# The same steps of a linear-attention and MLP-mixer kernel in another order of issue

## The chip, the cores and the metric

The kernel runs on one core of a Trainium2 chip. The metric is the device time in microseconds. The core has five instruction queues that each run strictly in their written order: TensorE (PE; its weight loads are shown as PEld), VectorE (DVE), ScalarE (ACT), GpSimd (POOL) and SyncE (SP), which here issues all DMA transfers. Semaphores tie the queues together.

## What is computed

The first half is a delta-rule recurrence over 768 tokens, for 4 batch elements with 8 heads of 48 features; the second is a mixer on its output. Cut to what matters:

```python
k_n = k / (norm(k, axis=-1) + 1e-06)
for t in range(S):                                    # 768 tokens
    y[:, :, t] = einsum('bhd,bhde->bhe', q[:, :, t], state)
    v_old = einsum('bhde,bhd->bhe', state, kt)
    state = state + bt[..., None] * einsum('bhd,bhe->bhde', kt, vt - v_old)
x = y.transpose(0, 2, 1, 3).reshape(B, S, H * D)      # (4, 768, 384)
h = maximum(x.transpose(0, 2, 1) @ w_tok1, 0) @ w_tok2   # 768 -> 256 -> 768
u = x + h.transpose(0, 2, 1)
out = u + maximum(u @ w_ch1, 0) @ w_ch2               # 384 -> 1536 -> 384
```

All data are float32 on the chip (the mixer's weights arrive as 64-bit floats and are rounded there).

## The kernel before

**Chunks.** The recurrence is done in chunks of 64 tokens: 12 per element, 48 in all (`r0` to `r47`). Two chunks make a unit `u` of 128 tokens (24 units). Inside a chunk the delta rule becomes the inverse of a triangular 64x64 matrix for each head, so that only the state goes from chunk to chunk. The inverses do not depend on the state and can be made ahead.

**Jobs and steps.** The kernel is written as some 280 Python generators, the jobs; each `next()` on one issues one step, a few instructions for one or two engines. A job's name is a letter and a number:

- `k` loads keys and queries of a unit (SP), `v` loads its values (SP) and scales them by the keys' norms on POOL (L426); a `v_st` tile has two buffers.
- `p` makes norms, scaled keys and the transposed keys and queries (`kq`); it uses ACT, DVE, POOL, and PE for units under 12; later units turn on DVE (L369).
- `c` and `d` are the grams `p_g` (PE L453) and their masking on DVE (L459).
- `t` hands the triangular blocks to the inversion. For the first six units engines copy them; later, four DMAs write them to `n_dram` (L628).
- `i0` to `i6` invert the 32x32 blocks of up to four units at once. From `i2` on its first step is a DMA that loads x from `n_dram` (L675); then come 30 steps of two DVE instructions, `sub` (L681) and `x` (L686), and the last one writes x to `w_dram` (L705). `f` fetches the inverses back (SP L653).
- `h` and `j` join the inverted blocks (PE `p_z`, `p_x`; ACT and DVE between).
- `r` is one chunk of the recurrence, ten steps numbered from 0: `p_k` from keys and state (PE L862, steps 0 to 3); `rest` = `p_k` - values (DVE L869, step 4); `p_y` and `p_w` (PE L882, L886, step 5); `w_t` (ACT L892, step 6); `p_s` and the rest of `p_y` (PE L900, L901, step 7); the new state `s_t` (DVE L909, step 8); the output (ACT L914, step 9). The first chunk of an element has no state and leaves out the first part.
- `m0` to `m3` are the mixers of the four elements: token matmuls `p_1` (PE L1060) and `p_h` (L1073), transposes `p_ut` (L1083), then for each of three pairs of token blocks the channel matmuls. For element 0 these are `p_c` (L1140, evicted by ACT); for the others a scheme with fewer products, `p_r` (L1032, evicted by ACT L1041 or added up by DVE L1044). The second channel matmul is `p_o` (L1162), added to the result by DVE (L1091) and stored by SP (L1094). The mixer has three PSUM tiles of its own.
- `w` loads and rounds pieces of the weights (SP, ACT, DVE, POOL), `s` forms sums of them on DVE, `b` loads beta, and `x`, `z` and `Y` are filler matmuls on zeros that write a PSUM tile of their own (L225, L235).

**The order.** A long string lists the steps: 2,543 of them, `name*n` for n steps in a row. A loop calls the jobs in that order, and since scheduling is manual, each engine's queue holds its instructions in exactly this order. So a step's place is its place on every queue that it uses: a `rest` listed behind a step of an inversion waits on DVE until that one is through. Tile buffers are given out and freed in this order too.

**What ties the order.** `r` of a chunk needs `j` of its unit (the joined inverse), `v` (scaled values) and the state of the chunk before. `m0` needs all twelve chunks of element 0 for its token matmuls, of which two chunks feed one step. `p` of unit u from 12 on overwrites the `kq` of unit u - 6, so it waits until the recurrence has read that. Assertions in the generators state these ties at build time.

Of the kernel before, what the change touches and what calls it, by code (L numbers as in the profile page):

```python
# [23 lines left out]
def kernel(  # L24
# [149 lines left out]
    t11 = const.tile([128, NB, HB], FP32, name="t11")  # L174
# [17 lines left out]
    w2 = const.tile([128, NDH, S], FP32, name="w2")  # L192
# [20 lines left out]
    def place(u):  # L213
        return NV + u if u < 2 else (u - 2) % NV
# [194 lines left out]
    def stacked(dst, src, u):  # L409
        rows = heads_of(src, u)  # L410
        for par in range(2):
            for cc in range(2):
                nc.sync.dma_start(
                    out=dst[PAR[par ^ cc], :, cc], in_=rows[par, cc]
                )
                yield

    def load_v(u):
        vsts[u] = v_st = loads.tile([128, NP, 2, D], FP32, name="v_st")
        yield from stacked(v_st, v, u)  # L420
        assert u in masked
        nrm = nrms[place(u)]
        nc.gpsimd.tensor_tensor(
            out=nrm, in0=nrm, in1=eps[:, :, None].to_broadcast([128, NP, 2]), op=ALU.add
        )
        nc.gpsimd.tensor_tensor(  # L426
            out=v_st, in0=v_st,
            in1=nrm[:, :, :, None].to_broadcast([128, NP, 2, D]), op=ALU.mult,
        )
        scaled.add(u)  # L430
        yield
# [121 lines left out]
    t16 = spare[:, cuts[1] : cuts[2]].rearrange("s (q t b) -> s q t b", q=2, t=QB)  # L553
# [688 lines left out]
    c1*2 d1 k2 p2*2 c1 t0 d1 c1*2 d1*3 t0 p2*8 c2*2 w2 d2 c2*3 Y d2 w2 k3*6 p3 d2*2  # L1242
    p3 d2 t1*3 x p3*7 c3 k4*5 k7 w13 w18*2 d3*2 v1*2 v0*2 c3*3 v0 c3 d3*3 t0 p4*2
    t2*3 x t3*2 p4*2 x t3 i0*2 w13 p4*2 w18 w17*2 i0 k4 i0*9 p4 i0*2 p4*2 c4 k8
    c4*3 w13*2 w6*2 k5*2 v0 k6 k5*2 i0*2 d4*2 k5 x z d4*3 c4 z*2 p5*2 k5 t4 p5 h0
    h1 h0 w8*2 h1 Y i0 f0 Y p4 f1 h2*2 p5*3 f0*2 w6 h0*5 k6*5 p6 z f2*2 k8*3 p5 w6
    p5 p3 p5 j0*3 f1*2 h1*5 j0*2 w8*2 w17 f2 h2*3 v0 t4*2 w17 r0*5 p6 h2*2 c5*2 v1
    w11*2 j1 p5 k7*2 c5 k7 c5 r0 c5 r0*2 w14*2 v1 w11*2 k7*2 p7 d5*5 r1*5 w14*2
    p6*2 t5 j1 t5*2 r1*2 j1 j2 p7 h3*2 r1*3 p6*3 i1*2 r2*5 k8*2 f3*2 w9 k9*3 j1*2
    v2*2 i1*3 j2*2 r2*2 f3 i1*2 p6*3 w16 v2 w16*3 r2*2 h3 r2 i1 d6 r3*5 i1*2 w9*3  # L1250
    v2 d6 h3 v2 w0 h3*2 r3 h3 d6*2 w0 d6 j3 c6*5 r3*4 w0 j2 w0 p8*2 j2 r4 p8 r4*4
    k9*3 j3*2 r4*2 i1*2 w24 i1*2 p7*7 r4 c7 r4 r5*5 k10 p9 k10 p9 c7 r4 c7*3 i1
    w5*2 p7 r5*2 w24*3 r5*3 j3*2 i1 r6*4 w26 v3*5 p9 k11 r6 d7*5 w26*3 p8*3 t6*2
# [8 lines left out]
    k12*3 m0*4 c10 m0*2 w25 m0 w12 d10 f6*4 f7*2 p11*2 m0*3 w12 w21 w12 p12 p11*2  # L1262
    m0*2 f7 w21*2 j6*2 j7 v6 p12 w25*3 f8*2 w27*2 m0 j6 j7*2 m0 r12*5 f8 f7 j8*2
    r12 m0 w23*4 j8 r12 t10 r12 t10*2 r13 p10 w23 r13*4 w20*2 p11*3 p12*2 w20*2
    f9*2 w32 f9 j9 f9 r13*2 f8 m0 r13 t10 r13 w31 w32 c11 w32 w23 w32 w31 p11 c11
    w31 d11 v8*3 r13 k13 c11 v8 c11*2 w30*2 w31 d11 r14 v8 d11 r14 d11*2 k13*6 r14
    t11 p12*2 k13 w29 r14*2 k13 m0 w30*2 k13*3 m0*4 r14*2 t11*2 c12*3 w29 c12*3 t12
    w33 r14*2 p12 t12 r14 t11 m0 w23 p13*3 r15 w25 t12*2 r15*4 m0 p13*3 k14*2 r15
    p13 r15 m0*4 k14*4 w33 k14*2 r15*3 c13*6 t13*2 w33 t13*2 i3 w31 r16*4 v9 k14*4
    w31 m0*2 r16 w33*3 j9 w27 v9 m0*2 j9 r16*2 w25 w31 m0 r16*2 j9 p14*3 r17*5 p14  # L1270
    r16 w33 m0 p14 k15*2 m0 v9 k15*2 i3*3 v10 i3 v9 m0*2 i3*3 m0*2 i3*2 p14 r17 p14
    i3 m0 i3 r17*4 i3 m0*6 i3*2 p13 i3*9 k15*3 j9 k15*2 p15 v9 i3*2 r18 i3 r18*2
    v10*2 k15*3 i3*5 r18*2 p15 v10 m0*2 f10*3 f11 m0*4 f11 m0*3 f11 f10 m0*4 r18
    f13*2 c14*6 f12*2 r18*4 m0*2 f12 m0 s p15 r19*5 j10 m0 r19*2 j10*2 s r19 p15*3
    r19*2 p14 f11 m0 j11*2 j12 r20 v10 r20*2 j11 r20*2 k16*6 p15 k16 m0*2 k16*2
    m0*2 r20 c15*2 k16*2 f13 r20 v11 c15*3 k16 v11 c15 v11 r20*3 p16 s v11 p16 m0*2
    r21*3 p15 r21*2 p16*4 j12 j13 k17*3 r21 j12 r21 p16 k17*3 m0*3 r21*3 m0 r22*2
    k17 r22 v11 k17 r22 k17*3 c16*4 r22*3 m0 c16*2 r22*3 t15 m0 r23*4 s p17*2 r23
    p16 p17*3 m0 p17 r23 k17 p17 t16 p17 m0*2 t16*2 t14*3 c17*2 t16 c17*3 r23 t14
    r23 c17 m0*2 s m0*3 t15*3 t17 s*4 t17*3 s*2 k18 m0*3 f12 i4*2 r23 i4*3 m0*2 i4  # L1280
    m0*2 v12*4 i4*2 k18 v12 k18*2 i4 k18 j13 m0*2 j13 r24*5 f13 j13*2 i4*4 r24 m0
    k18 m0*2 k18*2 v13*2 k18*2 r24 i4*2 k18*2 p18*2 i4 m0*3 r25 p18*2 r25*3 p18 i4
    k19 i4 k19 i4 k19*4 i4*2 m1 r25 m1*5 r24 r25 i4*8 k19*2 v14*4 i4 m1 v13*2 i4*2
    m1*2 p18*2 r25*2 m1 r25 m1 r25 p19*2 m1*3 r26*3 v13 r26*2 m1 c18*4 m1*2 r26*2
    m1*2 c18*2 m1*2 r26 m1 r26 m1*3 r27*2 k19*2 r26 k19*2 f14*3 r27*2 f14 j14*2
# [59 lines left out]
```

## Time and profile before

| what | value |
|---|---|
| runs of the kernel | 638.67, 640.15 and 643.08 us (median 640.15) |
| span of the profiled execution, first to last instruction | 636.9 us |
| PE busy | 608.5 us (96%), 9132 matmul passes |
| DVE busy | 447.9 us (70%) |
| ACT busy | 268.0 us (42%) |
| POOL busy | 107.2 us (17%) |
| mean granted clock of PE | 0.976 |
| DMA moved by the kernel's queue | 48.89 MB in 135,680 packets |

The profiled execution's time beside its span is not shown apart; the three runs are from 1.8 to 6.2 us longer than the span. In the profile a float32 matmul shows as two passes, a transpose as one. "Idle before" in brackets is how long an engine stood still before an instruction, and what released it. The granted clock (PEclk) is the share of PE's full speed in a stretch. A `q` behind an engine's name (SPq) is its instruction queue: issuing DMAs.

### The profile page before, as it was taken

The page shows a single profiled execution, that of the slowest core. Times are in us where ns is not written, and L with a number is a line of the kernel's source. Part 1 is how long each engine was busy: PE and PEld are TensorE (multiplying, and loading weights), DVE is VectorE, ACT ScalarE, POOL GpSimd, SP SyncE. Part 2 cuts the span into 40 slices and gives each one's busy share as a digit, 9 for nine tenths or more (in the row PEclk, how much of TensorE's full clock was granted, in tenths as well). Part 3 has the DMA queues.
Part 4 walks back from the last instruction along what each step waited for, and adds up shares of the span by engine and source line. Part 5 has one row for each costly group of instructions (what it writes and reads, how often), then busy time and mean ns, then how long its engine had stood idle before and what let it go on. Part 6 is the DMA issues. An engine that isn't in the chain of part 4 may idle for free.

```text
span 636.9 us, 21542 instructions
## 1 busy us (share of the span) xinstructions
PE 608.5 (96%) x9132; PEld 531.5 (83%) x9132; DVE 447.9 (70%) x1132; ACT 268.0 (42%) x693; POOL 107.2 (17%) x146
## 2 busy tenths in 40 slices
PE   8488988899999999999999999999999999999997
PEld 5367877668898988859889999769999987999997
DVE  4987876967999658988969987776728253373643
ACT  7758785447523342215624323325334130232240
POOL 2348354235210211111111001000010000000000
PEclk9978796999999999999999999999999999999999
DMA  9686666666543355344454223202020000000000
GB/s 201 127 148 151 153 142 153 162 135 162 110 113 89 71 116 101 76 109 79 90 103 95 43 82 58 48 5 42 5 53 2 27 2 0 26 1 26 2 26 26
DMA packets 135776, 50.27 MB, mean 79 GB/s; under 512 B 114656, under 2 KB 130144, under 8 KB 135680
## 3 DMA queue, kind: packets, MB, share of 16 engines
q1 hardware_dynamic: 135680, 48.89, 35.2%
q8 instruction: 72, 1.18, 0.8%
q14 instruction: 24, 0.20, 0.1%
HBM read 39.42 MB, written 9.44 MB: 77 GB/s over the span
## 4 chain that ended last, share of the span: by engine, by line
PE 82%; DVE 7%; ACT 4%; DMA 3%; issue 2%; POOL 1%; SPq 1%; ACTq 0%; DVEq 0%; POOLq 0%
PE p_o L1162 26%; PE p_r L1032 20%; PE p_c L1140 8%; PE p_h L1073 5%; PE p L1060 4%; PE p_k L862 3%; PE p_g L453 3%; PE p_y L882 3%; PE p_s L900 3%; PE p_w L886 1%; DVE sub L681 1%; DVE x L686 1%; PE p_y L901 1%; PE p_ut L1083 1%; PE p_z L785 1%
## 5 line engine op out<-in xcount | busy, mean ns | idle before, releaser
L1162 PE MATMUL p_o<-wc,r 128*128 128x192 f32 x720 | 126.1, 329 | 0.6 <-ACT u_t L1087 0.6
L1162 PEld LDWEIGHTS p_o<-wc,r 128*128 128x128 f32 x720 | 116.8, 190 | 2.7 <-ACT u_t L1087 1.1
L1044 DVE TENSOR_TENSOR r<-r,p_r 128x512 f32<-128x512 f32 x90 | 59.8, 684 | 38.1 <-PE p_r L1032 34.3
L1091 DVE TENSOR_TENSOR xb<-xb,p_o 128x192 f32<-128x192 f32 x84 | 29.3, 350 | 57.8 <-PE p_o L1162 57.3
L1041 ACT COPY r<-p_r 128x512 f32<-128x512 f32 x54 | 31.3, 585 | 85.7 <-PE p_r L1032 76.1
L686 DVE TENSOR_TENSOR x<-x,sub 128x84 f32<-128x84 f32 (+24 forms) x178 | 59.4, 334 | 6.1
L681 DVE TENSOR_TENSOR sub<-x 128x84 f32<-128x84 f32 (+24 forms) x178 | 58.0, 326 | 6.8 <-DMA x<-n_dram 2.3
L1162 PE MATMUL p_o<-wc,s 128*128 128x192 f32 x288 | 51.5, 331 | 0.3 <-DVE xb L1091 0.3
L1140 PE MATMUL p_c<-u_t,wc 128*128 128x256 f32 x216 | 51.0, 386 | 0.2 <-ACT u_t L1087 0.2
L1162 PEld LDWEIGHTS p_o<-wc,s 128*128 128x128 f32 x288 | 46.7, 190 | 1.4 <-DVE xb L1091 0.6
L1048 ACT ACTIVATE r<-r 128x512 f32<-128x512 f32 x54 | 34.0, 631 | 26.7 <-DVE r L1044 26.2
L426 POOL TENSOR_TENSOR v_st<-v_st,nrm 128x384 f32<-128x384 f32 x24 | 20.1, 838 | 146.3 <-DMA v_st<-in_v_dram 109.3
L1140 PEld LDWEIGHTS p_c<-u_t,wc 128*128 128x128 f32 x216 | 39.7, 190 | 6.0 <-ACT u_t L1087 0.4
L516 POOL TENSOR_TENSOR mb<-mask_c,cs 128x512 f32<-128x512 f32 x20 | 21.2, 1062 | 138.9 <-DVE cs L494 138.6
L914 ACT ACTIVATE xb<-p_y 64x192 f32<-64x192 f32 x96 | 31.2, 325 | 23.6 <-PE p_y L901 12.2
L892 ACT COPY w_t<-p_w 128x192 f32<-128x192 f32 x48 | 15.2, 316 | 58.0 <-PE p_w L886 57.5
L1032 PE MATMUL p_r<-u_t,wc 128*128 128x128 f32 x288 | 38.7, 277 | 0.0
L453 PE MATMUL p_g<-kq 48*64 48x128 f32 (+1 forms) x704 | 33.6, 281 | 3.8 <-ACT kq L529 3.3
L1032 PE MATMUL p_r<-t_d,wc 128*128 128x128 f32 x288 | 37.3, 280 | 0.0
L1032 PEld LDWEIGHTS p_r<-u_t,wc 128*128 128x128 f32 x288 | 35.3, 192 | 0.4
L1060 PE MATMUL p<-xb,w 128*128 128x384 f32 x96 | 34.9, 511 | 0.0
L1032 PEld LDWEIGHTS p_r<-t_d,wc 128*128 128x128 f32 x288 | 34.0, 192 | 0.8
(184 smaller groups left out, 1212.2 us busy)
## 6 DMA issues: line engine op xcount, KB each, us to landing
d<-in_moe_w_ch_dram SPq DMA_DIRECT2D x24, 384.0 KB, 3.5
v_st<-in_v_dram SPq DMA_DIRECT2D x96, 48.0 KB, 2.7
out_dram<-xb SPq DMA_DIRECT2D x23, 192.0 KB, 1.9
kst<-in_k_dram SPq DMA_DIRECT2D x64, 48.0 KB, 2.9
n_dram<-gm SPq DMA_DIRECT2D x72, 32.0 KB, 2.4
pads<-in_k_dram SPq DMA_DIRECT2D x24, 96.0 KB, 2.9
pads<-in_q_dram SPq DMA_DIRECT2D x24, 96.0 KB, 2.9
gm<-w_dram SPq DMA_DIRECT2D x72, 32.0 KB, 2.1
```

Source lines behind the costliest of these rows:

```text
L453: nc.tensor.matmul(p_g[PAR[i ^ cc], p], kqt[f, p, cc, 0], kqt[f, p, cc])
L681: nc.vector.tensor_tensor(out=tmp, in0=y[:, :, 0:s, s : s + 1].to_broadcast([n, k, s, w]), in1=y[:, :, s : s + 1, s + 1 : m].to_broadcast( ...
L686: nc.vector.tensor_tensor(out=y[:, :, 0:s, s + 1 : m], in0=y[:, :, 0:s, s + 1 : m], in1=tmp, op=ALU.add,)
L914: nc.scalar.mul(y[:, :, D * i : D * i + D], p_y[PAR[1 - i]], 1.0 if c else -1.0)
L1032: nc.tensor.matmul(p[:, i], pieces[i // width][:, at : at + 128], f[f"u{n}"], start=first and i == 0, stop=True, skip_group_check=True,)
L1041: nc.scalar.copy(o, p)
L1044: nc.vector.tensor_tensor(out=o, in0=o, in1=p, op=ALU.add if sign > 0 else ALU.subtract)
L1048: nc.scalar.activation(o, o, ACTF.Relu)
L1060: nc.tensor.matmul(p_1[dh], piece_of(w1, c, 0)[:, dh * 128 : (dh + 1) * 128], xb[:, c], start=(c == 0), stop=(c == NCH - 1),)
L1073: nc.tensor.matmul(p_h, piece_of(w2, j, c * 128)[:, c * 128 : (c + 1) * 128], r1[j], start=(j == 0), stop=(j == NDH - 1),)
L1140: nc.tensor.matmul(p_c[:, k], piece_of(wc1, cb, f * 128)[:, f * 128 : (f + 1) * 128], u_t[:, cb], start=(cb == 0), stop=(cb == NCB - 1),)
L1162: nc.tensor.matmul(p, a[:, m], wc2[:, m, j], start=(start and i == 0), stop=(i == NM - 1), skip_group_check=True,)
```

## The change

The order string is replaced from the 186th of its 2,543 steps on (the 181st by the change's own count); the first 185 stand as they did, and each job is called exactly as often as before, the fillers included. No instruction, shape or buffer is changed. One assertion goes, which said that a unit's values may be scaled only after its blocks went to the inversion; in the new order v6 stands ahead of t6.

The fork lies within `i0`. By steps, the ends of r5, r11, r23 and r35 lie at 488, 772, 1355 and 1973 before and at 485, 767, 1320 and 1974 after; `i2` covers 649 to 780 before and 666 to 780 after; `m0` begins at 674 and 644, `m3` at 2352 and 2338.

The core of the diff: the assertion, the part of the order in which i2 and r9 to r12 stand, and its end.

```diff
     def load_v(u):
         vsts[u] = v_st = loads.tile([128, NP, 2, D], FP32, name="v_st")
         yield from stacked(v_st, v, u)
-        assert u in masked
         nrm = nrms[place(u)]
...
-    w29 w27*2 r8*2 w29*3 j4*2 r8 w22*4 t9*4 r8*3 p10 h5*2 k11 h5 j5 Y i2 r9*3 r8
-    r9*2 i2*4 j5 i2*3 r9*2 i2 h5 k12*2 j5 Y r9*2 m0 v6 k11 j5 p9 w4*2 r10*3 i2*2 j5
-    k10 r10 p10*4 w4 v5 i2 v5*3 r9 k11*2 v5 r10*3 i2 w4 i2*3 w15*3 w19*2 i2 w19 m0
-    i2 w12 r10*2 m0*2 r11 r10 p11 k12*4 w19 p11 p10 k12*2 p12 Y i2 w25 r11*3 d10*4
-    r11*2 v7 c10*3 w15 k12 i2*2 w21 i2*4 v6*3 r11*2 i2*3 k11 r11 v7*4 i2*4 c10
...
+    k11 d8*5 p9 v6*2 w28*4 f5*2 h4*5 j4 r7 t7 r7 p9*3 k9 p9*2 r7*2 w7*4 w27 t6
+    t7*3 r7 c9*5 d9*4 r8*3 p9 w27 d9 j4*2 r8 v4*3 h5 v4*2 r8 w29*4 h5 j4*2 p10 t8
+    p10 Y*2 t8*3 h5*2 j5 w27 r8*2 w27 r8 m0 w22*4 r8 r9 r8 p10*2 r9*3 t9*4 r9*4 h5
+    i2*3 p10*5 i2 j5 k12*4 r9 x i2 w4 i2*5 w4*3 r10 r9 m0*2 i2*4 r10 w19*2 v5
+    r10*2 k12*4 v5 m0 p12 j5*3 k11*2 w12 m0 v5*2 p12 i2 v5 w15*2 k12 r10*3 i2*2
+    k12*3 p12 k11*2 p11 d10 w19*2 w15 r10*2 r11*2 w15 r11*3 r10 v7 c10*3 r11 i2*7
+    r11*3 m0*2 w21 i2*2 v7*2 i2*6 w12 m0*2 d10*3 c10*2 d10 t10 m0*5 w12*2 p11*9
...
-    v23*3 m2 r46*4 m2*2 v23*2 r46 m2*9 r46*2 m2*2 r46*3 m2*7 r47*5 m2*6 r47 m2 r47
-    m2*2 r47 m2*6 r47 m3*6 m2*5 m3*6 m2*11 m3*3 m2 m3*159
+    r45*5 m2 r45*2 m2*4 r45*3 m2*3 r46*4 m2 r46*2 m2 m3 r46*3 m3 r47*5 r46 m2*4 m3
+    r47 m3 r47*3 m3*9 m2*11 m3*3 m2 m3*4 m2*2 m3*154
```

More of the change, by code (lines that the diff above doesn't have):

```diff
@@ new lines @@
+    p10 Y*2 t8*3 h5*2 j5 w27 r8*2 w27 r8 m0 w22*4 r8 r9 r8 p10*2 r9*3 t9*4 r9*4 h5
[3 more added lines that the diff above has]
+    r11*3 m0*2 w21 i2*2 v7*2 i2*6 w12 m0*2 d10*3 c10*2 d10 t10 m0*5 w12*2 p11*9
+    w25 w21*2 f6*3 w21 f7 m0*2 f7*2 m0 f6 j6*2 w25 j7 w27*2 w25*3 Y w29 j6 j7*2
+    m0*2 w23*2 f8*3 j8 w23*3 r12*4 t10*3 f7 j8 r12 p12 j8 r12*3 m0 r13*6 c11*4 f9
@@ new lines @@
+    i4*7 m0*4 j13 r24*5 p16 j13*2 k18*12 i4*4 v13 r24 m0*3 i4*3 m0*2 i4*2 r24 i4
+    m0*3 r25*4 p18*6 r25 i4 r24 i4*8 v14 m1*6 v14*3 r25 m1 p18 r25*2 p18 r25 k19*4
+    m1 r25 k19*5 p19 i4*6 m1*6 s v13 f14*3 r26*4 f15 r26 c18*2 r26 c18 m1*4 c18*3
+    p19 r26*4 m1*3 f14 m1 j14 m1*3 r27*4 j14 r27*2 p19*3 r27 j14 p19 m1*4 f15*3
+    j15 r27*3 k19*2 j15*2 v14 r28*3 k19 r28*2 p19*2 s*2 f16*2 f17 m1*5 k20*4 r28
+    c19*6 k20*4 r28*4 p20 k20*2 p20*2 m1*2 p20 m1*4 r29*4 p20*2 r29 v15*4 m1*4 f16
+    k20*2 r29 p20 r29 m1*6 r29*3 t19 j16 k21*11 v15 r30*5 t18*4 f16 j16 m1 k21
```

101 lines of the change are left out of this document (42 added, 59 removed).

## Prediction

> **What bounds the kernel now.** I read the page first (busy shares, the slices, the chain by engine), then a table of busy time over stretches, then the chain in order of time, then the timeline of the places where the chain leaves PE.
>
> ```profile
> span 636.9 us, 21542 instructions
> PE 608.5 (96%) x9132; PEld 531.5 (83%) x9132; DVE 447.9 (70%) x1132; ACT 268.0 (42%) x693; POOL 107.2 (17%) x146
> ...
> PE   8488988899999999999999999999999999999997
> ...
> PEclk9978796999999999999999999999999999999999
> ...
> PE 82%; DVE 7%; ACT 4%; DMA 3%; issue 2%; POOL 1%; SPq 1%; ACTq 0%; DVEq 0%; POOLq 0%
> ```
>
> PE is busy for 96% of the span, and the slices show that what it lacks lies in the first eight. The next rows (columns: stretch, its length, then busy time and count of PE, PEld, DVE, ACT and POOL, the granted clock, DMA share, GB/s) split the span there.
>
> ```profile
> 126.00:160.00 34.00, 33.41 (x467) 24.30 (x468) 25.09 (x62) 19.74 (x55) 13.95 (x16) 1.00 0.65 151
> 160.00:600.00 440.00, 437.54 (x6171) 391.61 (x6163) 310.57 (x788) 151.97 (x391) 38.36 (x55) 1.00 0.26 57
> 600.00:637.00 37.00, 33.67 (x242) 32.98 (x240) 14.42 (x29) 7.30 (x12) 0.00 (x0) 1.00 0.06 22
> ```
>
> From 126 us to 600 us PE idles 0.6 + 2.5 = 3.1 us. So after 126 us the time is PE's own work, and an order can change only how that work is packed. Ahead of 126 us it is the recurrence of the first element: the mixer of that element can run without pause once step r11 (the last chunk of the element) is done. In the trace r11 forms its `rest` at 123.10, and the first dense mixer matmuls follow at 125.5. The last steps up to there are these (timeline of DVE: start, duration):
>
> ```profile
> 105.14 0.36 DVE L869 TENSOR_TENSOR rest<-p_k,v_st 128x192 f32<-128x192 f32 x1 [0.53 <-PE p_k L862]
> 106.62 0.19 DVE L681 TENSOR_TENSOR sub<-x 128x30 f32<-128x30 f32 x1 [1.12 <-DMA x<-n_dram]
> ...
> 111.50 0.35 DVE L909 TENSOR_TENSOR s_t<-s_t,p_s 128x192 f32<-128x192 f32 x1
> ...
> 115.14 0.34 DVE L869 TENSOR_TENSOR rest<-p_k,v_st 128x192 f32<-128x192 f32 x1
> ...
> 121.53 0.34 DVE L909 TENSOR_TENSOR s_t<-s_t,p_s 128x192 f32<-128x192 f32 x1
> ...
> 123.10 0.35 DVE L869 TENSOR_TENSOR rest<-p_k,v_st 128x192 f32<-128x192 f32 x1
> ```
>
> One chunk's `rest` to the next one's takes 10.0 and 8.0 us here. Between them DVE works without a pause at the third inversion (i2, L681 and L686), which it began at 106.62. So from 106.6 us to 123.1 us the path is DVE's queue, in its written order.
>
> **The change part by part.** The steps are the same, each as often as before, so nothing is added to or taken from any engine. I counted by the two orders what stands ahead of chosen steps, and priced each step by its own rows in the trace. For DVE most of it is the inversions, whose groups on the page are:
>
> ```profile
> L686 DVE TENSOR_TENSOR x<-x,sub 128x84 f32<-128x84 f32 (+24 forms) x178 | 59.4, 334 | 6.1
> L681 DVE TENSOR_TENSOR sub<-x 128x84 f32<-128x84 f32 (+24 forms) x178 | 58.0, 326 | 6.8 <-DMA x<-n_dram 2.3
> ```
>
> (a) Up to r11. DVE work ahead of r11's `rest`: 109.3 us before, 106.0 us after, since i2 has then gone 16 of its sub-steps and not 18. That is -3.3 us. ACT's work ahead of it stays (106.4, 106.3). At r3's end the sums are within 1.3 us of each other, at r8's `rest` DVE has 1.6 us less ahead and ACT 2.3 us less. Against it stands SP. The four loads of v6 and other loads now stand ahead of the last `n_dram` write of the third round (t9): six more DMAs. The rows (SP issue, count, and the chain's DMA pieces):
>
> ```profile
> 97.20 1.79 SPq L628 DMA_DIRECT2D n_dram<-gm  x4
> 99.04 0.60 SPq L413 DMA_DIRECT2D lent<-in_k_dram  x1
> 102.28 0.34 SPq L675 DMA_DIRECT2D x<-n_dram  x1
> ```
>
> ```profile
> 98.54 3.54 DMA n_dram<-gm
> 102.28 4.33 DMA x<-n_dram
> ```
>
> At 0.60 us an issue, six are +3.6 us for i2's load if SP has no slack, and nothing if it has. The rows show SP waiting 2.6 us, from 99.64 to 102.28. Bounds of (a) are thus -3.3 and +3.6; a gain beyond -3.3 is not excluded where r9 and r10 now stand in a better place among i2's sub-steps, so I stretch it to -5. I take -2.0, nearer the DVE sum, because DVE is what the chain runs on there, with a third of the SP price laid on it.
>
> The removed assertion issues nothing. It only lets v6 (its DMAs and its two POOL operations) go ahead of t6. In both orders v6 holds one of the two `v_st` buffers until r13, so v4 and v5 share the other one. After the change v5's four DMAs stand among six loads and one weight load on SP; about 10 us of issues lie between i2's load and v5's last DMA. By the new order r10's `rest` is due about 12 us after that load's landing, some 16 us after its issue, so v5 is hidden; if SP waits there for more than 3 us, r10 waits.
>
> (b) Mixer work that now stands ahead of r11: PE work ahead of r11's `rest` is 69.6 us before and 70.6 after (the first element's token matmuls go earlier). What is left behind is 1.0 us less: -1.0.
>
> (c) Alternations on PE. Rows of the chain in order of time, in which one kind of large matmul runs unbroken:
>
> ```profile
> 303.34 1.09 PE p_r L1032 x8
> ...
> 306.73 1.98 PE p_r L1032 x16
> ...
> 309.32 2.88 PE p_r L1032 x24
> ...
> 577.44 13.67 PE p_r L1032 x120
> ```
>
> From 8 to 24 a pass costs (2.88 - 1.09) / 16 = 0.112 us, and 8 of them are 0.90, so every unbroken run costs 0.19 us beside its work. By the two orders there are 86 runs of large matmuls behind r11 before and 77 after: 9 x 0.19 = -1.7.
>
> (d) Handovers in the recurrence. Each chunk has three: `p_k` to DVE's `rest` to `p_w`; `p_w` to ACT's `w_t` to `p_s`; `p_s` to DVE's `s_t` to the next `p_k`. PE must have other work in between. Where it has none:
>
> ```profile
> 319.98 0.22 PE L886 MATMUL p_w<-rest,gm 64*64 64x48 f32 x1
> 320.65 0.25 PE L900 MATMUL p_s<-w_t,gm 64*64 64x48 f32 x1 [0.46 <-ACT w_t L892]
> ```
>
> Start to start this is 0.67 us, so a handover with less PE work than about 0.75 us in it loses the difference. A group of grams covers one (0.89 for 32 passes):
>
> ```profile
> 302.00 0.89 PE p_g L453 x32
> ```
>
> Counting the PE work inside each of the handovers from r12 on, before has 12 short ones that lack 3.0 us in all, after has 22 that lack 7.0 us (r13 with all three of its own, r29 and r30 with nothing at all at their ends). So +4.0. The least is 0, where DVE and not PE limits at those places; the most is about +6, with 0.1 us more for each of the 22.
>
> (e) The loads of the inversions. A step of an inversion stands on DVE and waits for its x to land: from the last `n_dram` write to landing it was 106.62 - 99.0 = 7.6 us for i2. Behind it in DVE's queue stand the `rest` and `s_t` of the recurrence and the additions that free the mixer's PSUM tiles, so PE follows a few us later. The PE work between the last write and the first DVE step, in issue order, is 3.1, 10.2, 2.0, 10.3 and 11.0 us for i2 to i6 before, and 1.4, 2.0, 2.0, 3.9 and 2.8 after. What it costs now:
>
> ```profile
> DVE sub L681 <- DMA x<-n_dram: 2.3, 2, 1.1
> ```
>
> All five inversions together wait 2.3 us, though i4 has 2.0 us of cover already: SP runs ahead of the other engines there. So the nearest row says no more than 1.2 us of DVE time for a short cover, and PE has mixer matmuls for that. I take 0, with +8 as the far end (worked out under the rivals).
>
> (f) The clock. The table of stretches again, now cut at the changes of the clock:
>
> ```profile
> 50.10:60.30 10.20, 8.38 (x303) 7.69 (x298) 7.19 (x15) 8.77 (x26) 8.95 (x12) 1.00 0.86 203
> 60.30:70.60 10.30, 10.30 (x245) 9.30 (x242) 8.20 (x22) 7.74 (x21) 3.63 (x5) 0.50 0.51 118
> 70.60:80.80 10.20, 8.87 (x315) 7.64 (x311) 8.68 (x27) 8.84 (x29) 4.56 (x6) 1.00 0.63 150
> ...
> 91.00:101.30 10.30, 8.52 (x268) 7.16 (x263) 7.01 (x15) 9.68 (x26) 6.71 (x8) 1.00 0.74 173
> 101.30:111.50 10.20, 9.38 (x170) 7.26 (x165) 6.30 (x23) 3.94 (x14) 2.99 (x4) 0.50 0.61 146
> 111.50:121.80 10.30, 8.27 (x133) 5.39 (x132) 9.85 (x26) 5.83 (x15) 3.08 (x4) 1.00 0.64 163
> ```
>
> Twice behind the fork the clock falls to 0.50 for about 10.2 us, after stretches in which PE was busy for 82% and 83%; after 80% at 111.5 to 121.8 it did not. While it is down PE does 245 matmuls in the time of 315: (315 - 245) / 315 x 10.2 = 2.3 us. The new order can drop both (-4.6) or meet a third (+2.3). I take 0, since the fillers that keep PE busy are as many as before and the PE work ahead of every step is nearly the same.
>
> The Trainium skill, "TensorE: Matmul & The Clock Gate" (Part 1: The HAM clock gate), has the clock fall after an idle window of about 3.4 us. By that rule neither of these two falls should be there, because PE's longest wait ahead of the first is this one, and term (f) would be 0 with no spread; the trace disagrees (0.50 at 60.3 and 101.3), so the spread stays.
>
> ```profile
> 58.10 1.18 issue
> ```
>
> The sum: -2.0 - 1.0 - 1.7 + 4.0 + 0 + 0 = -0.7, so a span of 636.2 us. The three runs are 638.67, 640.15 and 643.08; the profiled span of 636.9 is 3.25 us under their median, and I lay that on: **639.5 us**, no change that can be told. A measurement of this kernel tells about 1% (6.4 us) from no change.
>
> **The rivals.** *Faster by over 1%.* The first element's path is shorter by more than the sum says. For it: DVE alone carries the path from 106.6 to 123.1, and 3.3 us of its work go behind r11. It needs (a) at -5 and both falls of the clock gone, -4.6, with (b) and (c) as above and the handovers of (d) at half, +2: -10.3, a span of 626.6, 630 us as a run; with one of the two falls left, 632. Against it: SP's six DMAs, and that the handovers inside r0 to r11 have less PE work in them, so PE idles more there and the clock may fall oftener.
>
> *Slower by over 1%.* DVE stands at an inversion's first step, waiting for x, with the recurrence and the additions behind it. Place: i3, i5 and i6, whose cover falls from over 10 us to 2.0, 3.9 and 2.8. If SP is not ahead, DVE waits 5.6, 3.7 and 4.8 us, and i2 6.2. The mixer has three PSUM tiles, and a step of eight `p_r` passes takes 1.09 us, so PE can go on for about 3 us: 2.6 + 0.7 + 1.8 + 3.2 = 8.3 us. With the rest of the sum that is +7.6, 647.8 us. It decides from a DVE wait of more than 3 us on. Against it: 2.3 us for all waits on x now.
>
> *Same, but for other reasons*: (a) positive and (d) small, ending within 1% too; it is in the forecast's range.
>
> **How the numbers follow.** Forecast (within 1%, 634 to 646): 0.50. Faster by over 1%, at about 631: 0.28, because the places where the path can shorten (DVE's queue, the clock) are seen in the rows. Slower by over 1%, at about 648: 0.22. The range takes both rivals in and leaves out a tenth on each side: 629 to 649. The likeliest case has its own range of 635 to 645.
>
> **What would show it.** (a) r11's `rest` at 120 to 122 us and not 123.1; wrong if i2's first step comes later than 107. (c) and (d): PE's idle time from 160 to 600 us at 5 to 7 us (2.5 now), on `w_t`, `rest` and `s_t`. (e) the wait of `sub` for x at under 4 us in all; over 12 us would be the slower rival. (f) two stretches at 0.50 behind 50 us. The forecast is wrong if the dense mixer starts outside 121 to 128 us, or if PE idles over 10 us behind it.

## The result, and the profile after

The changed kernel took 660.97 us (median of 4 runs, 659.96 to 662.0), the kernel before 640.24 us beside it: a ratio of 1.0327 (95% interval 1.0298 to 1.0357). On two later occasions the same changed kernel took 665.43 and 662.79 us (1.0414, 1.0379 to 1.045; and 1.0346, 1.0315 to 1.0378). So it is slower by 21 to 26 us where the forecast was no change, 639.5 us; the time lies outside its range of 629 to 649. Behind the assertion that went, line numbers of the changed file are one less than before: `sub` L680, `rest` L868, `s_t` L908.

The page of the changed kernel (span, busy shares, the slices of PE and of its clock, the chain that ended last):

```profile
span 660.1 us, 21566 instructions
...
PE 614.1 (93%) x9132; PEld 533.2 (81%) x9132; DVE 444.8 (67%) x1132; ACT 269.6 (41%) x693; POOL 107.9 (16%) x146
...
PE   8488788799999999999997999999999999999998
...
PEclk9979799889999999999998999999999999999999
...
PE 62%; DVE 14%; DMA 9%; ACT 5%; SPq 5%; issue 3%; POOL 1%; DVEq 0%; ACTq 0%; POOLq 0%
```

The work is the same by count (9,132 passes on PE, 1,132 instructions on DVE), and busy times are close (PE 614.1 for 608.5 us, DVE 444.8 for 447.9). PE stands still for 46.0 us where it stood for 28.4, and the chain that ended last runs on PE for 62% and not for 82%: DVE, DMA and SP's queue have taken its place. The table of stretches, cut as in the prediction:

```profile
126.00:160.00 34.00, 31.44 (x452) 23.08 (x443) 22.14 (x66) 16.17 (x47) 8.01 (x8) 0.85 0.41 95
160.00:600.00 440.00, 428.06 (x6160) 378.89 (x6159) 306.78 (x769) 151.58 (x394) 46.59 (x64) 1.00 0.27 60
```

PE's idle time from 160 to 600 us is 11.9 us (2.5 before; I had said 5 to 7, and over 10 as the mark of a wrong forecast). Ahead of it the first element ends late, as the timeline of DVE shows (the first line below is r8's `rest` in the kernel before, the others are the changed kernel):

```profile
98.85 0.36 DVE L869 TENSOR_TENSOR rest<-p_k,v_st 128x192 f32<-128x192 f32 x1
```

```profile
104.46 0.36 DVE L868 TENSOR_TENSOR rest<-p_k,v_st 128x192 f32<-128x192 f32 x1 [1.35 <-POOL v_st L425]
...
110.68 0.36 DVE L868 TENSOR_TENSOR rest<-p_k,v_st 128x192 f32<-128x192 f32 x1
111.52 0.31 DVE L680 TENSOR_TENSOR sub<-x 128x30 f32<-128x30 f32 x1 [0.48 <-DMA x<-n_dram]
...
125.27 0.36 DVE L868 TENSOR_TENSOR rest<-p_k,v_st 128x192 f32<-128x192 f32 x1 [2.62 <-POOL v_st L425]
...
129.85 0.36 DVE L868 TENSOR_TENSOR rest<-p_k,v_st 128x192 f32<-128x192 f32 x1 [1.20 <-PE p_k L861]
```

These are `rest` of r8, r9, r10 and r11 and i2's first step. r8's is already 5.6 us late and stands 1.35 us for v4's scaled values; i2 starts at 111.52 and not at 106.62; r10's `rest` stands 2.62 us until v5's values are scaled; r11's comes at 129.85 and not at 123.10. On SP the loads of v4 end 11 us later (the changed kernel's four, then the last two of the kernel before):

```profile
97.77 2.84 SPq L413 DMA_DIRECT2D v_st<-in_v_dram  x4
```

```profile
88.20 1.43 SPq L413 DMA_DIRECT2D v_st<-in_v_dram  x2
```

The last of them is SP's 105th issue, at 100.02, and was its 94th, at 88.85; the loads of v6 now stand ahead of it. Behind r10's `rest` stands a second wait (timeline of ACT):

```profile
125.75 0.57 ACT L277 ACTIVATE d<-d 128x384 f32<-128x384 f32 x1 [3.28 <-DMA d<-in_moe_w_ch_dram]
...
126.78 0.32 ACT L891 COPY w_t<-p_w 128x192 f32<-128x192 f32 x1
```

ACT stands 3.28 us for a weight load with r10's `w_t` behind it. So with v5 alone on time that `w_t` could hardly have come sooner. The table of waits (time in all, times, longest) of the changed kernel, cut:

```profile
ACT ksq L480 <- DMA kst<-in_k_dram: 18.6, 6, 7.4
DVE sub L680 <- DMA x<-n_dram: 13.3, 5, 5.1
...
PE p_k L861 <- DVE s_t L908: 5.0, 4, 3.5
PE p_w L885 <- DVE rest L868: 4.1, 6, 2.4
```

The wait of `sub` for x has gone from 2.3 to 13.3 us, over the 12 that I had named as the sign of the slower rival; ACT's wait for key loads (first line) was 1.3 us before. How such a wait reaches PE is seen at i5 (timeline of DVE, then of PE):

```profile
348.38 0.35 DVE L1090 TENSOR_TENSOR xb<-xb,p_o 128x192 f32<-128x192 f32 x1 [1.59 <-PE p_o L1161]
353.82 0.19 DVE L680 TENSOR_TENSOR sub<-x 128x30 f32<-128x30 f32 x1 [5.08 <-DMA x<-n_dram]
...
358.19 0.35 DVE L908 TENSOR_TENSOR s_t<-s_t,p_s 128x192 f32<-128x192 f32 x1
```

```profile
358.68 1.09 PE L861 MATMUL p_k<-s_t,kq 48*64 48x48 f32 x16 [3.48 <-DVE s_t L908]
```

DVE stands 5.08 us for x with r32's `s_t` behind it in its queue, then works off seven steps of i5, and PE waits 3.48 us for that `s_t`.

To compare kernels I use PE's lag: I add up the matmuls, each at what its kind takes at full clock, and see how much later than the kernel before a kernel has done the same sum. At five points of the old kernel (us 93, 135, 207, 331, 352) the changed one lags by 6.0, 10.1, 11.5, 16.9 and 22.6 us, and then by 22 to 23 to the end. In this trace there are three losses: some 10 us up to r11 and the mixer's start, 5 to 7 us around i3 and i4, 5.7 us at i5. The place of the third is not fixed. In the traces of the second and third occasion (f1 and g4 below) the lag grows by 2.6 and 0.6 us from 331 to 352, and by 3.8 and 5.8 us from 300 to 352 (5.8 in the first trace).

### The profile page after: what moved, and what is told of

The parts are those of the page before. It is cut to its first block, busy times and chain, and to the rows that moved or that the text cites. A ratio compares the mean times of both kernels' runs of the same rounds, so it can differ in the third digit from the quotient of the medians.

```text
span 660.1 us, 21566 instructions
## 1 busy us (share of the span) xinstructions
PE 614.1 (93%) x9132; PEld 533.2 (81%) x9132; DVE 444.8 (67%) x1132; ACT 269.6 (41%) x693; POOL 107.9 (16%) x146
## 4 chain that ended last, share of the span: by engine, by line
PE 62%; DVE 14%; DMA 9%; ACT 5%; SPq 5%; issue 3%; POOL 1%; DVEq 0%; ACTq 0%; POOLq 0%
PE p_r L1031 19%; PE p_o L1161 18%; PE p_h L1072 4%; PE p L1059 4%; DVE sub L680 3%; DVE x L685 3%; PE p_g L452 3%; PE p_k L861 3%; DMA x<-n_dram 2%; PE p_c L1139 2%; SPq L627 2%; PE p_s L899 2%; PE p_y L881 2%; DMA d<-in_moe_w_ch_dram 2%; DMA kst<-in_k_dram 1%
## 5 line engine op out<-in xcount | busy, mean ns | idle before, releaser
L680 DVE TENSOR_TENSOR sub<-x 128x84 f32<-128x84 f32 (+24 forms) x178 | 58.7, 330 | 17.9 <-DMA x<-n_dram 13.3
L452 PE MATMUL p_g<-kq 48*64 48x128 f32 (+1 forms) x704 | 37.9, 289 | 4.0 <-ACT kq L528 2.8
L458 DVE TENSOR_TENSOR gm<-p_g,mb 128x512 f32<-128x512 f32 x44 | 29.0, 686 | 10.7 <-PE p_g L452 10.3
L452 PEld LDWEIGHTS p_g<-kq 48*64 48x64 f32 (+1 forms) x704 | 28.5, 141 | 8.8 <-ACT kq L528 3.9
```

Of the source, the lines that this page charges most:

```text
L452: nc.tensor.matmul(p_g[PAR[i ^ cc], p], kqt[f, p, cc, 0], kqt[f, p, cc])
L680: nc.vector.tensor_tensor(out=tmp, in0=y[:, :, 0:s, s : s + 1].to_broadcast([n, k, s, w]), in1=y[:, :, s : s + 1, s + 1 : m].to_broadcast( ...
```

## The experiments

**Halves of the order: e1, e2, f4.** Everything up to a step in one order, what is left in the other:

```diff
e1, f4:
-    new order
+    new order up to step 8 of r11 (e1) or of r23 (f4), then the old one
e2:
-    old order
+    old order up to step 8 of r11, then the new one
```

> The new order up to the end of r11 (the last chunk of element 0), then the old order for all that is left. Theory (the loss sits in three places: the way to the dense mixer, the stretch of i3, and the wait for x at i5): the first place alone is in, so 8 to 10 us slower than the old order, 648 to 651 us. Rival (the loss is spread over the packing on TensorE behind r11, the ten more short handovers and the clock, and the start is neutral): within 3 us of the old order, 640 to 643 us.

Measured: 651.59 us, ratio 1.0181 (1.0159 to 1.0202), just over the theory's range. The start alone costs 11.8 us; the lag is 12.1 us at 135 and stays there (13.0 at 352).

> The old order up to the end of r11, then the new order for all that is left. Theory of three places: without the first place, so 11 to 14 us slower than the old order, 651 to 655 us, with the wait of i5 for x still there. Rival (spread over the packing behind r11): the whole 20 us stay, 658 to 661 us.

Measured: 660.86 us, 1.0314 (1.0279 to 1.035): 21 us, the rival's value. The two halves cost 33 us, the whole 21 to 26; they do not add. With the old start r11 is on time (PE does its work up to there 0.2 us later than before), yet i3's load of x goes out as late as with the new start. One reason is its place, 50 steps later in the new order (k3 below). From the chains of e2 and of the changed kernel, in that order:

```profile
188.02 4.66 DMA x<-n_dram
```

```profile
188.86 4.54 DMA x<-n_dram
```

And from SP's timeline of the kernel before:

```profile
176.35 0.34 SPq L675 DMA_DIRECT2D x<-n_dram  x1
```

On e2's way from r11 to i3 lie other waits, ACT's for instance (timeline of ACT and PE):

```profile
131.59 0.21 ACT L488 ACTIVATE nrm<-ksum 128x8 f32<-128x8 f32 x1 [5.40 <-POOL v_st L425]
...
132.56 1.65 PE L1072 MATMUL p_h<-r,w 128*128 128x384 f32 x2 [4.29 <-ACT r L1067]
```

ACT stands 5.40 us for POOL, with the mixer's eviction (the step that empties its PSUM tile) behind it, and PE 4.29. With a stretch of 3.41 us at half clock from 132.25 this makes the lag 6.3 us at 135. In the changed kernel, where r11 is late itself, the same `p_h` waits for nothing. So these 6 us are a cost of e2 that the whole order does not pay: at least half of the 7 to 12 us that the halves cost too much.

> The new order up to r23's step 8 (the new state of the second element's last chunk, step 1,321 of 2,543), then what is left in the old order. Theory (three separate losses: about 10 us up to us 145, 6 us from us 196 to 285 on i3 and i4, 5 to 6 us at i5): the first two stay but for what the old order mends behind r23, and the third goes: 652 to 656 us, with no wait of over 2 us at i5. Rival (what shows at i5 is the lag of SP's and DVE's queues that the new order has built up before, so that the old order would stand there too): 658 to 661 us.

Measured: 660.29 us, 1.0311 (1.025 to 1.0372), with 665.43 for the changed kernel on the same occasion: 5 us less, though the time lies at the rival's. Its lag goes from 19.6 to 20.6 us between 331 and 352, the changed kernel's by 2.6 on that occasion and by 5.7 in its first profile. From 300 to 352 it grows by 0.9 us, against 3.8 to 5.8 in the three traces of the changed kernel. So most of the loss there comes with the order behind r23.

**The changed kernel again: f1, g4.** No edit.

> The changed kernel itself, unedited, beside the three kernels that follow, since two kernels with the same first 1,700 steps (the one with i5's steps moved, and the one with v5's loads together) ran 1 to 3 us longer than it did. Every theory: 660 to 662 us. If it comes out at 663 or 664, the same steps run differently from one occasion to the next by that much, and the two earlier results are no slower than it.

> The changed kernel, unedited, as the measure for the two kernels with fillers, since it came out at 661.0 us on one occasion and at 665.4 us on another. Every theory: 660 to 666 us.

Measured: 665.43 us, outside the 660 to 662, and 662.79 us. The same program moves by 4 us from one occasion to another, so smaller differences between occasions mean nothing here.

**One wait taken away: e3, e4.**

```diff
e3:
-    t21 i5 v16 r32 j17 p21 m1*4 i5*7 k22*5 j17 k22*6 m1*2 j17 r32*2 j17 r32*2 m1*2
+    t21 i5 v16 r32 j17 p21 m1*4 k22*5 j17 k22*6 m1*2 j17 r32*2 j17 r32*2 i5*7 m1*2
e4:
-    w19*2 v5 r10*2 k12*4 v5 m0 p12 j5*3 k11*2 w12 m0 v5*2 p12 i2 v5
+    w19*2 v5*4 r10*2 k12*4 m0 p12 j5*3 k11*2 w12 m0 p12 i2 v5
```

> The new order with one change: the first seven VectorE steps of i5 stand behind r32's new state and not ahead of it and of a mixer addition. Theory (VectorE stands 5 us for i5's x, and r33 and the mixer stand behind it): TensorE's idle time of 3.5 us ahead of r33 and the short fall of the clock behind it go, 3 to 5 us less than the new order, 656 to 658 us. Rival (that wait is hidden, TensorE would idle there anyway): no change, 660 to 661 us.

Measured: 664.12 us, 1.0383 (1.0365 to 1.0402); missed. The wait of r33 for `s_t` is gone, and from 331 to 352 the lag grows by 2.6 us only, but it had reached 22.3 us before that place, and unedited (f1) it also grew by 2.6 us there. With 660.97 to 665.43 for the unedited kernel, no gain or loss can be told.

> The new order with the four loads of v5 together on the SP queue, ahead of four key loads, two others and a weight load that stood between them. Theory (r10's rest waits 2.6 us for v5, and the dense mixer starts that much later): 2 to 3 us less than the new order, 658 to 659 us, and r10's rest waits for i2's steps alone. Rival (r10 and r11 would wait for VectorE's work on i2 anyway, and key and weight loads that come later take the gain back): no change, 660 to 661 us.

Measured: 661.89 us, 1.0343 (1.0322 to 1.0364), close to the rival's value. r10's `rest` no longer waits for v5 and comes at 122.73, 2.5 us sooner. Its `w_t` then waits for the weight load on ACT, as in the changed kernel, and PE stands 1.61 us for it; the lag at 135 is 8.9 us all the same.

**The waits for x: f2, f3, k2, k3.** In f2, f3 and k2 the loads of x of i3 to i6 stand behind the first fetch of the round before and read that round's blocks; of the four moves the diff shows i3's in f2.

```diff
f2, f3, k2:
-        assert masked.issuperset(rounds[rnd])
+        assert rnd > 2 or masked.issuperset(rounds[rnd])
...
-            nc.sync.dma_start(out=x, in_=xins.pop(rnd)[0:n])
+            nc.sync.dma_start(out=x, in_=xins[max(rnd - 1, 2)][0:n])
...
f2:
-    w25 w21*2 f6*3 w21 f7
+    w25 w21*2 f6 i3 f6*2 w21 f7
...
k3 (old order):
-    c13 t13*2 w33 t13*2 i3 w31 r16*2
+    c13 t13*2 w33 t13*2 w31 r16*2
...
-    m0 p14 k15*2 m0 v9 k15*2 i3*3
+    m0 p14 k15*2 m0 v9 k15*2 i3*4
```

> The new order, but the loads of x of i3, i4, i5 and i6 do not wait for their round's blocks: each takes the n_dram of the round before, which was written long ago, and is issued right behind the first fetch (f) of the round before. So those inversions work on other data (this part of the computation is changed); steps, shapes and all else stay. It takes away DVE's standing for x at i3 to i6: 2.3 + 2.0 + 5.1 + 3.3 = 12.7 us in the trace of the changed kernel. Theory (PE's lag behind us 160 of 12 to 13 us comes from these waits, through DVE's queue): the lag stays at about 10 us up to us 195 and then hardly grows, 647 to 652 us. Rival (it comes from the handovers of the recurrence and from key and value loads that are listed too close to their use; the waits for x only lie beside): 657 to 661 us, with DVE and ACT waits elsewhere in place of those for x.

Measured: 658.23 us, 1.0293 (1.025 to 1.0336), 7.2 us less than the changed kernel on the same occasion. The waits of DVE in f2:

```profile
DVE rest L868 <- POOL v_st L425: 5.2, 3, 2.1
...
DVE sub L680 <- DMA x<-n_dram: 0.4, 1, 0.4
```

The waits for x are gone, and the lag at 135, 207, 331 and 352 is 9.7, 10.3, 14.8 and 15.2 us: the loss at i5 is gone, 4.5 us of the middle one stay. PE's idle time from 160 to 600 us falls from 11.9 to 6.5 us. The time lies at the rival's edge (657 to 661), since I had counted the whole loss behind 160 us as x's.

> The same edit to the old order (x of i3 to i6 from the n_dram of the round before, issued behind the first fetch of that round; the inversions work on other data): the control of the kernel above. There the waits for x sum to 2.3 us, and PE idles for 1.8 us behind us 126. Both theories: 637 to 641 us, no difference that can be told.

Measured: 639.11 us, 0.9985 (0.9959 to 1.001), as both said. The same edit is worth nothing where the waits are short.

> The old order up to r11's step 8, then the new one, and x of i3 to i6 from the n_dram of the round before (other data in those inversions). Without the last edit this order took 660.9 us, as long as the whole new order, though r11 was on time (rest at 123.3 us, 123.1 in the old order). Theory (with r11 on time it is SP's and DVE's queue that holds PE at i3 to i6): 649 to 654 us. Rival (the new order loses the time in the recurrence's handovers and in ACT's waits for weights, whatever x does): 656 to 661 us.

Measured: 655.33 us, 1.0248 (1.0201 to 1.0295), between the two; by the ratios it is 4 us under e2. So by this pair, from two occasions, the waits for x are a fifth of what the new rest costs by itself. The rest stays: PE's wait for ACT at the mixer's start is 4.68 us here, the lag is 7.3 us at 135, 12.0 at 300 and 16.0 at 331.

> The old order with one step moved: i3's load of x stands directly ahead of i3's first DVE step, 50 steps later, as in the new order. Theory that a short cover alone costs: DVE waits 4 to 5 us for x at 180 us, PE has some 3 us of mixer work for it, 641 to 644 us. Rival (the wait is short where SP runs ahead, and PE has work behind it): 638 to 641 us.

Measured: 646.36 us, 1.0129 (1.0079 to 1.0179): +7.8 us (5 to 11 by the interval) for one DMA issue that stands 50 steps later, more than the theory said. Its timeline (SP, DVE, then PE):

```profile
182.17 0.43 SPq L674 DMA_DIRECT2D x<-n_dram  x1
...
186.01 0.19 DVE L680 TENSOR_TENSOR sub<-x 128x30 f32<-128x30 f32 x1 [5.99 <-DMA x<-n_dram]
```

```profile
188.94 1.81 PE L1161 MATMUL p_o<-wc,r 128*128 128x192 f32 x5 [4.79 <-DVE xb L1090]
```

On SP the load now stands behind loads of keys and values and goes out at 182.17 and not at 176.35. DVE waits 5.99 us, the additions that free the mixer's tiles stand behind it, and PE idles 4.79. A stretch of 3.41 us at half clock follows (1.7 us): 6.5 us, and the lag goes from -0.6 to 5.6 us there and stays.

**The clock: g1, g2, g3, k4.** In all traces the clock changes on a grid of 3.413 us. The changed kernel's table of stretches, cut on that grid (granted clock third from the end):

```profile
65.12:68.54 3.42, 3.15 (x149) 2.87 (x149) 3.12 (x12) 2.86 (x9) 0.44 (x1) 1.00 0.89 222
68.54:71.95 3.41, 0.66 (x40) 0.53 (x33) 1.75 (x7) 1.63 (x4) 0.73 (x1) 1.00 0.92 214
71.95:78.78 6.83, 6.49 (x121) 6.32 (x121) 2.55 (x7) 3.94 (x12) 2.97 (x4) 0.50 0.40 74
...
123.16:126.57 3.41, 1.04 (x37) 0.82 (x36) 1.23 (x4) 0.82 (x2) 0.83 (x1) 1.00 1.06 233
126.57:136.81 10.24, 8.11 (x116) 6.26 (x114) 7.21 (x20) 3.44 (x11) 1.98 (x2) 0.50 0.25 59
...
355.26:358.67 3.41, 0.00 (x0) 0.02 (x1) 3.14 (x12) 0.52 (x1) 0.00 (x0) 1.00 0.63 134
358.67:362.09 3.42, 3.41 (x27) 3.33 (x28) 2.96 (x9) 0.79 (x3) 0.00 (x0) 0.50 0.44 137
```

Windows with PE busy for 0.66, 1.04 and 0.00 us are each followed by half clock. So I filled such places with matmuls on zeros:

```diff
g1 (new order):
-    v5 w15*2 k12 r10*3 i2*2
+    v5 w15*2 k12 r10 z x*2 r10*2 i2*2
...
-    w19*2 w15 r10*2 r11*2
+    w19*2 w15 x*2 r10*2 x r11*2
...
-    i2*7 r11*3 m0*2
+    i2*7 r11 x r11*2 x*2 m0*2
g2 (besides):
-    k9 i1*2 r2 w0*4
+    k9 i1*2 z r2 w0*4
...
-    p22 r33*3
+    p22 z*2 x r33*3
g3, k4 (old order; r10 and r11 alike):
-    t5*2 r1*2
+    t5*2 z r1*2
...
-    j4*2 r8 w22*4 t9*4 r8*2
+    j4*2 z r8 w22*4 t9*4 r8 x*2 r8
```

> The new order with nine more filler matmuls (one z of 128x512, eight x of 128x128, all on zeros and read by nobody) put into the places where PE stands still around r10 and r11: z and two x ahead of r10's step 5, two x ahead of r10's step 7, one ahead of r11's first step and one ahead of its step 7, two ahead of m0's step 5. In all runs so far the clock changes only on a grid of 3.413 us, and of 18 such windows in which PE was busy for under half, 17 were followed by a fall to 0.50; over 0.8 only 2 of 1,450 were. In the changed kernel such a window (0.31) stands at 123.2 us, and the 10.2 us at half clock behind it fall into the dense mixer, where they cost 5.1 us. Theory (the wait at r10 is paid twice, once as idle time and once through the clock): no stretch at 0.50 between 124 and 145 us, and 4 to 6 us less than the changed kernel in this call. Rival (the clock falls there anyhow, or PE has slack there): within 2 us of it.

Measured: 662.92 us, 1.035 (1.0305 to 1.0396), with 662.79 for the unedited kernel on the same occasion: the rival's value. First the unedited kernel's stretches there, then those of g1:

```profile
120.07:123.48 3.41, 0.90 (x5) 0.23 (x3) 1.47 (x4) 0.00 (x0) 0.65 (x1) 1.00 0.89 216
123.48:137.13 13.65, 10.95 (x149) 8.16 (x150) 8.43 (x23) 5.71 (x15) 2.16 (x3) 0.50 0.37 66
```

```profile
126.22:129.63 3.41, 2.34 (x72) 2.02 (x72) 2.57 (x8) 2.23 (x7) 0.97 (x2) 1.00 0.81 125
129.63:146.70 17.07, 16.49 (x145) 10.55 (x145) 14.50 (x41) 4.78 (x14) 2.36 (x3) 1.00 0.31 86
```

The fall is gone, as the theory said, and the end has not moved: the lag at 135 is 8.5 us (9.5 without the fillers, which take PE's time themselves), at 352 it is 24.9. What was gained up to the mixer is lost at i3 (DVE, then PE, of g1):

```profile
195.57 0.19 DVE L680 TENSOR_TENSOR sub<-x 128x30 f32<-128x30 f32 x1 [6.00 <-DMA x<-n_dram]
```

```profile
197.38 1.50 PE L1161 MATMUL p_o<-wc,r 128*128 128x192 f32 x5 [3.24 <-DVE xb L1090]
```

DVE's wait for i3's x is 1.78 to 2.92 us in the three traces of the unedited kernel. It is 6.00 us here, 4.76 in g2 and 4.60 in e4: the three edits that leave less lag at 135 (8.5, 6.6 and 8.9 us, where the unedited kernel has 9.5 to 13.2).

> The kernel above with four more fillers: one z ahead of r2's step 7, where PE stood for 2.75 us at 69.1 us with nothing waited for, and z, z, x ahead of r33's first step, where it stood for 3.49 us at 355.2 us behind i5's wait for x. Each was followed by a stretch at 0.50 (6.8 and 3.4 us). Theory: these falls go too, 3.4 + 1.7 us more, so 8 to 11 us less than the changed kernel in this call. Rival: the two places are not limits of PE, and each filler of over 1 us costs its own time: the same as the kernel above, or up to 2 us more.

Measured: 661.38 us, 1.035 (1.0298 to 1.0401); missed, no gain that can be told. Its four runs are 657.6, 660.4, 662.4 and 666.1 us at a mean clock of 0.984, 0.982, 0.974 and 0.972. That the clock makes this spread of 8 us is not shown: in g4 the lowest clock, 0.966, goes with the shortest run, 661.49 us.

> The old order with six more fillers: z ahead of r1's step 5 (PE stood for 1.18 us at 58.1 us), z ahead of r8's step 5 (0.78 us at 99.6), two x ahead of r8's step 7, z ahead of r10's step 5 (0.91) and of r11's first step (0.93). The falls at 60.3 and 101.3 us follow windows with PE busy for 0.65 and 0.75. Theory (these falls too come from the windows ahead of them, and their 10.2 us lie on the path): they go, 634 to 638 us, faster than the old order. Rival (they come from too many small matmuls, not from standing still, and the fillers cost what they take, up to 5 us): 639 to 644 us.

> The old order with six fillers, unedited from the first time, which came out at 0.9972 of the old order with an interval of 0.9944 to 1.0001; with five rounds it should tell whether it is faster than both kernels. Theory (the falls of the clock that it takes away lie in part on the path): 0.996 to 0.999. Rival (the fillers cost what the clock gives): 0.999 to 1.002.

Measured: 638.87 us, 0.9972 (0.9944 to 1.0001), then 640.48 us, 1.0011 (0.9984 to 1.0038). The mean clock rises from about 0.977 to 0.987 (g3) and 0.985 (k4), and the time stays, which is the rival's value: the fillers cost what the clock gives. No version beats the kernel before.

**All at once, and SP's queue: k1, n1, n2.**

```diff
k1:
-    new order
+    new order with the edits of f2, e4 and g2
n1, n2 (n2 with f2's edit besides; two more places, of v6 and k12, not shown):
-    r6*2 p8*2 v6*2 p8*4 r6*3 p8 h4*2 i1 h5*2 f5 f4*3 r7*3 c8*2 r7*2 v6 c8*3 k11
+    r6*2 p8*2 v6 p8*4 r6*3 p8 h4*2 i1 h5*2 f5 f4*3 r7*3 c8*2 r7*2 c8*3 k11
...
-    i2*4 r10 w19*2 v5 r10*2 k12*4 v5 m0 p12 j5*3 k11*2 w12 m0 v5*2 p12 i2 v5 w15*2
+    i2*4 r10 v5 r10*2 v5 m0 j5*3 k11*2 m0 v5*2 i2 v5 w15*2
-    k12 r10*3
+    r10 v6*4 k12*6 p12*2 k12 w19*2 w12 r10*2
```

> The new order with everything mended that a run has pointed to so far, at once: x of i3 to i6 from the n_dram of the round before (other data in those inversions), v5's four loads together, and the 13 fillers ahead of r2's step 7, around r10 and r11 and ahead of r33. Alone, the first gave 7 us, the second and the fillers nothing that can be told in the end time, though the fillers took the fall of the clock at r10 away. Theory (each loss is hidden as long as another one ends later: SP's and DVE's queue holds PE at i3 to i6, and only with that gone do r10 and the clock count): 648 to 653 us. Rival (what is left is the packing of the recurrence and the mixer in the new order, which none of these touches): 655 to 659 us, as with the first alone.

Measured: 660.11 us, 1.0295 (1.0235 to 1.0355); the theory fails, and so does the rival by a little. The waits for x are gone, but the lag is 10.8 us at 135, 12.5 at 207 and 19.8 at 331.

> The new order with 11 DMAs moved behind r10's rest, to about where the old order has them: v6's last three loads (and its first scaling on POOL), k12's steps 2 to 8 with p12's first two, w19's first two and w12's first. In the new order 132 DMAs stand on SP up to v5's last load, 120 in the old one; that load went out at 119.6 us against 109.6, and r10's rest stood at 125.3 against 115.1. Theory (up to r11 it is SP's queue that is late, and v5 with it): v5's last load at 110 to 114 us, r10's rest at 116 to 121, r11's at 123 to 127; the end moves less, as other losses take over behind it: 657 to 662 us. Rival (r10 is late for other reasons, v5 just behind them): r10's rest stays at 123 or later, the end at 661 to 666.

Measured: 662.78 us, 1.0344 (1.0298 to 1.039), missed: the end and r11's `rest` (128.74) lie past the theory's ranges. v5's last two loads go out at 112.29 (SP's timeline of n1; below it that of the changed kernel):

```profile
112.29 1.72 SPq L413 DMA_DIRECT2D v_st<-in_v_dram  x2
```

```profile
119.00 1.26 SPq L413 DMA_DIRECT2D v_st<-in_v_dram  x2
```

So the delay of v5 is SP's queue, as expected. v4's last load still goes out at 98.55 only (100.02 without the edit, 88.85 in the kernel before). r10's `rest` comes at 122.09, between theory and rival, and its next step meets the wait for a weight (n1, DVE, ACT and PE):

```profile
122.09 0.35 DVE L868 TENSOR_TENSOR rest<-p_k,v_st 128x192 f32<-128x192 f32 x1
...
124.65 0.55 ACT L277 ACTIVATE d<-d 128x384 f32<-128x384 f32 x1 [1.51 <-DMA d<-in_moe_w_ch_dram]
...
126.03 0.34 PE L899 MATMUL p_s<-w_t,gm 64*64 64x48 f32 x1 [2.55 <-ACT w_t L891]
```

ACT stands for a weight load that SP has issued late; `w_t` of r10 is behind it, and PE waits 2.55 us. The lag at 135 is 10.2 us as before.

> The kernel above with x of i3 to i6 taken from the n_dram of the round before, behind that round's first fetch (other data in those inversions); that edit alone took 658.2 us, where the new order took 665.4 in the same call. Theory (SP's queue up to r11 and the waits for x are the two larger losses, and with the second gone the first counts): 650 to 655 us. Rival (the first stays hidden behind the packing of the rest): 656 to 660 us.

Measured: 655.9 to 665.91 us over four runs. The ratio, without the longest, is 1.0303 (1.0225 to 1.0381), 659.0 us: within the rival's range, and too wide to tell more. Its only trace is of the longest run, so whether the first loss stands in the others is not shown.

## Why the prediction was wrong

**Step (e), the loads of the inversions, failed most plainly.** I took 0, because all five inversions waited 2.3 us with 2.0 us of cover at i4, "SP runs ahead of the other engines there". Which inversions had waited I left open. The two waits were 1.12 us at i2 and this one at i5, whose cover was 10.3 us (timeline of DVE before):

```profile
334.07 0.19 DVE L681 TENSOR_TENSOR sub<-x 128x30 f32<-128x30 f32 x1 [1.15 <-DMA x<-n_dram]
```

i4 did not wait at all, and in the changed kernel, with the same 2.0 us of cover, it waits 2.03 us. So PE's work between the write and the first step does not tell the wait; k3 shows that the load's place on SP does. f2 prices the term at 7 us, k2 against e2 at 4, each give or take some 4 by the intervals. k3 gives a size without any of the other changes: 7.8 us for i3 alone, where my rival had 2.6 for it. The rival's mechanism (DVE stands, recurrence and additions stand behind it) is the one seen. It was undersized twice: PE's own work ran out sooner than 3 us (in k3 PE stands 4.79 of DVE's 5.99 us), and the clock fell behind the gap.

**Step (a), up to r11, failed next.** It was to give 2.0 us and loses about 10. I summed DVE's work and found 3.3 us less of it; DVE had less to do and waited more. On SP I had seen six more DMAs ahead of t9 and laid a third of their price on. Ahead of v5's last load stand 132 issues for 120, 88.9 for 81.1 us of issue; the load goes out 10.1 us later, and so does r10's `rest`. I had written that r10 waits if SP is held up there, and did not follow it; that SP holds r8 up by way of v4, I did not see. n1 shows that SP's place for v5 is real and not the whole: with v5 sooner, ACT's wait for a weight is next. No run with the new start takes the 10 us away (the least lag at 135 is 6.6 us, in g2), so how they divide among these waits stays open.

**Step (b)** falls with it: the first element's last token matmuls ran from 133.9 us, outside my 121 to 128.

**Steps (c) and (d)** summed to +2.3. With the waits for x gone (f2), PE's idle time from 160 to 600 us is 6.5 us, within the 5 to 7 that I had named. By the tables of waits 3.7 us of it are on `rest`, `s_t` and `w_t` (0.9 before): +2.8 where (d) had +4.0, so that mechanism is there. The lag grows by 4.5 us between 207 and 331; how much of that is (c) or other waits, no run separates.

**Step (f)**: the sum over the run was right (mean clock 0.976 and 0.977), but by luck: three falls of 6.83, 10.24 and 3.41 us happen to last as long as the two of 10.24 before. Where they fall was not foreseen: 10.24 us at half clock from 126.57, in the mixer's start, where before they lay at 101 to 111. g1 and g2 show that this did not set the end. My stretches of 10 us also hid what goes ahead of a fall: in the last window of 3.41 us ahead of the two old falls PE was busy for 0.65 and 0.75 of it, not for 82 and 83%.

**Why the losses do not add.** The larger waits found here are instructions that need a DMA, or the work behind one, standing ahead of the recurrence in an engine's queue: `sub` on DVE, weights and `nrm` on ACT, `v_st` on POOL. Taking one away lets the next one bind: e4, g1, g2, e3, n1 and k1 each removed a wait or a fall and kept the time. The next wait is seen in the traces for e4 and n1 (the weight on ACT) and for e4, g1 and g2 (i3's x); for e3 and k1 it is inferred. Two ends stay open. No run with the new rest comes back to 640 us: the nearest, k2, has the old start and no waits for x, and takes 655.33. And no run put SP's whole old order beside the new order of the other engines, so whether SP's lateness up to r11 begins in its own order or with the waits ahead of it is not shown; at v4 its own order has 11 more issues, 6.1 of the 11.2 us.

## What to carry to other kernels

When only the order changes, count for each DMA-fed step the issues ahead of its load on the issuing queue and the instructions behind the waiting one on its own engine; a short wait in the old trace says how far the queue was ahead there, and no more. One load 50 steps later (7.8 us in k3) cost more here than all my counted handovers (4.0). In a kernel with several in-order queues, judge a mended wait by the end time: the next one is often as late.

## What the runs showed of the hardware

The clock goes by windows. In 19 traces of this case (all but n2's), from 45 to 600 us, of 31 windows of 3.413 us at full clock with PE busy for under half, 29 were followed by half clock; of some 180 with 0.5 to 0.8 busy, 34; of some 2,780 above that, 3. A half-clock stretch lasts whole windows (3.4, 6.8, 10.2 or 13.7 us, once 17.1). The Trainium skill, "TensorE: Matmul & The Clock Gate" (Part 1: The HAM clock gate), has a free-running window of that length, and the grid agrees; but a gap of 2.37 us was enough where it lay within one window, so the rule of thumb of 3.4 us of idle time is too mild here.

In eight of these traces, all with the new start, PE stands still inside r2's step 7, always at the same matmul and for 1.5 to 3.2 us, with nothing waited for (2.75 us in the changed kernel, timeline of PE):

```profile
71.89 0.21 PE L900 MATMUL p_y<-w_t,wc 64*64 64x48 f32 x1 [2.75 <-issue]
```

In e1 and in the third run of the changed kernel (g4), with the same steps up to there, the stall is not seen. What PE waits for, no view here shows.
